# The first layer's low weights of 19 agents, made in four column parts of 128 columns instead of two products of 512

## The chip, the core and the metric

The kernel runs on one core of one Trainium2 chip. The metric is the device time of one execution in microseconds; lower is better. Engines are named as in the profile: PE (TensorE matmul; PEld is its weight load), DVE (VectorE), ACT (ScalarE), POOL (GpSimd) and SP (SyncE, which issues most DMAs).

## The reference

The reference is an attention over 49 agents, followed by a mixture of eight experts with the best one taken for each token:

```python
# q, k, v: (4, 11456, 128); agents: (4, 49, 128)
agent_v = softmax(scale * agents @ k.T) @ v        # 49 x 128 per batch
x = softmax(scale * q @ agents.T) @ agent_v        # 45824 tokens x 128
e_idx = argmax(x @ w_gate, axis=1)                 # eight experts
for e in range(8):                                 # tokens of expert e
    h = maximum(x[mask] @ w1[e], 0.0)              # 128 x 1024
    out[mask] = gate_w * sigmoid(x @ w_output_gate)[e] * (h @ w2[e])
```

## The kernel before, in words

There are four batches of 11456 tokens. For each batch the kernel computes the agents' values (49 rows of 128). It then picks the expert that most tokens of the batch should choose (`choose`, L878), and folds the agents' values into that expert's first layer: W = agent_v @ w1[e], 49 x 1024. With it a token's hidden values come from its 49 attention weights, and x itself is never formed. Tokens that chose another expert are collected in leftover tiles of 128 and computed again with their own expert: 13 such tiles for batches 0 to 2 and one for batch 3 (`left_static`, L1643). A scatter writes their rows over the first result (`left_scatter`, L1675); it begins for a phase only when all main tiles of the phase are stored.

W is made in float32 and then split into a high and a low part of float16. The tile `ad` (128 columns) holds the agents' values as its columns: 49 for the high part, the same 49 again for the low part, and the first 30 columns of the 49 last ones, so that one product with 128 rows serves three combinations of high and low. The remaining 19 agents (`AR`, 49 - 30) need another product. They lie in the tile `ar` of before in four groups of 32 columns, 19 of them filled, so that the 19 rows turn up four times, at partitions 0, 32, 64 and 96. `products` (L954) makes four products for each batch, each 128 rows by 512 columns: for each half of the 1024 columns one with `ar` and one with `ad`. Each takes a bank of PSUM, named aw. `first` (L971) turns each bank into float16: ACT writes the scaled high part (whi), DVE subtracts and writes the weights (w). The result of an `ad` bank is kept with that of the `ar` bank of its half (`rest`) in `state[b]["w"]`.

A main tile is 512 tokens. `mm1` (L1216) computes one half of its hidden values: four products h with the weights of `ad`, into four banks, and then four more that add the 19 agents, one in each group of 32 partitions of `rest`. Group g reads only its own 128 columns of the 512, at partitions 32g to 32g + 18 (L1230). `relu` splits the hidden values into a high and a low part (hh on ACT, hl on DVE), and `mm2` multiplies both with the second layer's weights vv into y. `finish` (L1270) adds the two parts of y (ACT ys, DVE os), and `store` (L1287) scales on POOL and issues the store to out on SP.

The order of the work is planned while the program is written. A `Clock` (L56) keeps a virtual time for each engine, with a cost for each instruction (`cost`, L169). `main_stream` (L1301) writes the main products and calls `tick` (L465) between them, which lets waiting streams of small work add an instruction when the plan says that its operands are ready. If nothing of the main stream is ready, `idle` (L510) adds small work or a product `warm` without a use. A change of cost anywhere changes the plan of all that comes later. Each engine then runs its instructions in the order written.

In batch 0 nothing of the main stream runs until its weights are there. There `products` uses banks of its own for the first two products, and waits after the first one until the sum of squares of w1 (mw_r) has been written; that sum sets the scale s1 (`first_scale`, L849). A similar sum, mv_r, sets the scale of the second layer (`second`, L998).

Of the kernel before, what the change touches and what calls it, by code (L numbers as in the profile page):

```python
# [7 lines left out]
F32 = mybir.dt.float32  # L8
F16 = mybir.dt.float16
# [257 lines left out]
def agent_attention_top1_moe(ctx, tc, qT, kT, v, aT, wg, wo, w1, w2, cst, out):  # L267
# [31 lines left out]
    def bank(name, dt=F32, w=512, k=None):  # L299

        k = last[0] = first_free()[1] if k is None else k
        t = ps.tile([P, w], dt, tag=f"b{k}", bufs=1, name=name)
        banks[k][1] = t.name
        return t
# [22 lines left out]
    def wait_free(long=False):  # L327
        while True:
            long_held[:] = [x for x in long_held if not banks[x[0]][0] and banks[x[0]][1] == x[1]]

            keep = clk.started and (long or not (Y or resting[0]))
            if n_free() > keep and not (long and len(long_held) > 1) and first_free()[0] <= clk.now() + 50.0:
                return
            yield None
# [43 lines left out]
        e16s.append(t)  # L378
    avd = []
    for i in range(2):  # L380
        t = cp.tile([P, 2, P], F32, name=f"avd_{i}")
        POOL.memset(t[:, 1, :], 0.0)
        avd.append((t[:, 0, :], t[:, 1, :].rearrange("p (g a) -> p g a", g=G4)))
    gss = []
    for i in range(2):
        t = cp.tile([P, 2, 18], F16, name=f"gs_{i}")
# [491 lines left out]
    def choose(b, x, ad=None, ar=None):  # L878

        sa = wk.tile([P, 1], F32, name=f"sa{b}", tag="sa")  # L880
        yield from DVE.q.tensor_reduce(sa, x, axis=AX.X, op=ALU.add)
        wgs = wk.tile([P, E], F32, name=f"wgs{b}", tag="wgs")
        yield from DVE.q.tensor_scalar(wgs, wgo[:, 0:E], sa, None, op0=ALU.mult)
        yield from wait_free()
        ga = bank(f"ga{b}")
        mark = hold()
        yield from PE.q.matmul(ga[:, 0:E], ones, wgs, start=True, stop=True)
        if ad is not None:
            yield from ACT.q.copy(ad[:, A:2 * A], ad[:, 0:A])
            yield from ACT.q.copy(ad[:, 2 * A:P], ad[:, AR:A])  # L890
            yield from POOL.q.tensor_copy(ar[:, :, 0:AR], ad[:, 0:AR].unsqueeze(1).broadcast_to([P, G4, AR]))
        gm1 = wk.tile([P, 2], F32, name=f"gm1{b}", tag="gm1")
        yield from DVE.q.tensor_reduce(gm1[:, 0:1], ga[:, 0:E], axis=AX.X, op=ALU.max)
        r1 = wk.tile([P, E], F32, name=f"r1{b}", tag="r1")
        yield from DVE.q.scalar_tensor_tensor(r1, ga[:, 0:E], gm1[:, 0:1], rank8, op0=ALU.is_ge, op1=ALU.mult)
        release(mark)
        yield from DVE.q.tensor_reduce(gm1[:, 1:2], r1, axis=AX.X, op=ALU.max)
        ei = wk.tile([P, 1], I32, name=f"ei{b}", tag="ei")
        yield from DVE.q.tensor_scalar(ei, gm1[:, 1:2], -1.0, float(E), op0=ALU.mult, op1=ALU.add)
        picking[0] = True  # L900
        urgent[0] = False
        state[b] = dict(w=[], vv=[])
        if ad is not None:
            spawn(gates(b, ad), -1)
        yield from SY.wait(ei)
        er = nc.values_load(ei[0:1, 0:1], engines=[SP], min_val=0, max_val=E - 1,
                            skip_runtime_bounds_check_because="eight minus a rank of one to eight")
        w1t = wk.tile([P, F], F32, name=f"w1t{b}", tag="w1t", bufs=2)
        yield from SY.q.dma_start(w1t, w1[bass.ds(er, 1)].rearrange("a p f -> p (a f)"))
        w2t = wk.tile([P, F], F32, name=f"w2t{b}", tag="w2t", bufs=2)  # L910
        yield from SY.q.dma_start(w2t, w2[bass.ds(er, 1)].rearrange("a p f -> p (a f)"))
        if b == 0:
            for x in (w1t, w2t):
                clk.ready[x.name] += 1000.0
        spawn(picked(w2t), -1)
        ndom = wk.tile([P, E], F32, name=f"ndom{b}", tag="ndom")
        yield from DVE.q.tensor_scalar(ndom, rank8, gm1[:, 1:2], None, op0=ALU.not_equal)
        state[b]["ndom"] = ndom
        return w1t, w2t
# [33 lines left out]

    def products(b, ad, ar, w1t, aw, marks):  # L954

        for hf in range(2):
            for x in (ar.rearrange("p g a -> p (g a)"), ad):
                while marks and b > 0 and "s1i" not in state[b]:
                    yield None
                own_ = b == 0 and hf == 0  # L960
                if not own_:
                    yield from wait_free()
                while own_ and not banks[len(marks)][0] or b == 0 and len(marks) == 1 and "mw" not in state[b]:
                    yield None

                t = bank(f"aw{b}_{len(marks)}", k=len(marks) if own_ else None)
                marks.append(hold())
                yield from PE.q.matmul(t, x, w1t[:, hf * 512:(hf + 1) * 512], start=True, stop=True)
                aw.append(t)

    def first(b, aw, marks, s1):  # L971


        s1d = wk.tile([P, 1], F32, name=f"s1d{b}", tag="s1d")
        yield from DVE.q.tensor_tensor(s1d, s1, dup, op=ALU.mult)
        for n in range(4):
            while len(aw) <= n:
                yield None
            hi = wk.tile([P, 512], F16, name=f"whi{b}_{n}", tag="whi", bufs=2)
            w = wk.tile([P, 512], F16, name=f"w{b}_{n}", tag=f"w{n}")  # L980
            yield from ACT.q.activation(hi, aw[n], AF.Copy, scale=s1d if n % 2 else s1)
            yield from DVE.q.scalar_tensor_tensor(w, aw[n], s1, hi, op0=ALU.mult, op1=ALU.subtract)
            release(marks[n])
            if n % 2:
                state[b]["w"].append((w, rest))
            else:
                rest = w

# [227 lines left out]
    def mm1(i, hf):  # L1216

        b, u, h, pp, n = tiles[i]
        w = pp * n
        own_, rest = state[b]["w"][hf]  # L1220
        x1, x2 = (x[:, 512 * h:512 * h + w] for x in X1[b, u])
        p = []
        for g in range(G4):
            p.append((bank(f"h{i}_{hf}_{g}", k=g), hold()))
            PE.matmul(p[g][0][:, 0:w], own_[:, g * P:(g + 1) * P], x1, start=True, stop=False)
            if g < G4 - 1:
                tick()
        for g in range(G4):
            rows = slice(32 * g, 32 * g + AR)
            PE.matmul(p[g][0][:, 0:w], rest[rows, g * P:(g + 1) * P], (x2 if g else x1)[rows, :], start=False, stop=True)  # L1230
        for g in range(G4):
            spawn(relu(i, G4 * hf + g, *p[g]), 0)
        tick(0)
        block()
        if hf == 1 and 4 * h + n == UNITS[u][2]:
            for x in ("x1", "x2"):
                scored((x, b, u))
        tick(0)
# [543 lines left out]
```

## Time and profile before

| what | value |
|---|---|
| median of 3 runs | 988.72 us (988.49 to 990.02) |
| profiled execution, its time | 988.17 us |
| profiled execution, its span | 986.2 us |
| PE busy | 958.7 us (97%) |
| DVE busy | 796.4 us (81%) |
| ACT busy | 592.3 us (60%) |
| first main product h | 56.81 us |
| last main product y | 972.17 us |
| last scatter issued on POOL | 977.79 us |
| mean granted clock of PE | 0.995 |

The span runs from the first instruction to the last; the execution's time includes what lies around it. A row of the timeline gives start, duration, engine, line, operation, output and inputs, size and count, and in brackets how long the engine had been idle and what it waited for. All instructions are recorded at one line, L217, because a helper issues them; they are told apart by the names of their tiles. A float32 product is recorded as two matmuls.

### The profile page before, as it was taken

What the parts mean: (1) busy time and instruction counts of PE and PEld (TensorE: products, weight loads), DVE (VectorE), ACT (ScalarE), POOL (GpSimd) and SP (SyncE); (2) the same over time, 40 slices, a digit from 0 to 9 for tenths busy, and PEclk for the clock granted to TensorE, in tenths of its full rate; (3) what the DMA queues carried; (4) which work ended last, traced back from release to release, by engine and by line L of the source; (5) the groups of instructions that cost most, each with busy time, mean ns of one, the idle gap of its engine ahead of it and who ended that gap; (6) DMA issues with size and microseconds to landing.
All of it is one profiled execution on the core that took longest, in us unless ns stands there. A gap on an engine that the chain in (4) does not pass through costs nothing. (4 is left out here: it accounts for less than half of the span.)

```text
span 986.2 us, 37446 instructions
## 1 busy us (share of the span) xinstructions
PE 958.7 (97%) x15695; PEld 730.3 (74%) x15695; DVE 796.4 (81%) x2122; ACT 592.3 (60%) x1404; POOL 353.5 (36%) x630
## 2 busy tenths in 40 slices
PE   9999999999999999999999999999999999999996
PEld 7866777777777777776777777777777677877785
DVE  2888888889788878789888888889999867767662
ACT  2376666665756666656666666657566555655552
POOL 1113264452233455331323553522225244544121
PEclk9999999999999999999999999999999999999998
DMA  9996556645467465444557545435532335633411
GB/s 328 307 301 163 157 140 152 166 133 155 116 194 199 131 160 144 140 153 129 150 170 190 155 135 155 128 120 113 134 86 83 110 111 164 178 126 120 133 32 67
DMA packets 108897, 148.62 MB, mean 151 GB/s; under 512 B 62594, under 2 KB 71222, under 8 KB 108724
## 3 DMA queue, kind: packets, MB, share of 16 engines
q1 hardware_dynamic: 107380, 144.70, 51.4%
q8 instruction: 124, 2.03, 0.9%
q0 software_dynamic: 1344, 1.49, 0.8%
q14 instruction: 49, 0.40, 0.1%
HBM read 90.88 MB, written 35.17 MB: 128 GB/s over the span
## 5 line engine op out<-in xcount | busy, mean ns | idle before, releaser
L217 PE MATMUL y<-vv,hh 128*128 128x256 f16 (+1 forms) x2880 | 527.5, 273 | 9.0 <-DVE lL L217 3.6
L217 DVE SCALAR_TENSOR_TENSOR hl<-h,hh 128x512 f16<-128x512 f32 (+1 forms) x736 | 449.3, 668 | 95.0 <-ACT hh L217 92.8
L217 PE MATMUL y<-vv,hl 128*128 128x128 f16 (+1 forms) x2880 | 500.6, 219 | 0.8 <-DVE hl L217 0.2
L217 ACT ACTIVATE hh<-h 128x512 f16<-128x512 f32 (+1 forms) x736 | 373.4, 590 | 195.6 <-PE h L217 191.4
L217 PEld LDWEIGHTS <-hh 128*128 128x128 f16 (+1 forms) x2880 | 282.8, 98 | 60.6 <-issue 18.4
L217 PEld LDWEIGHTS <-hl 128*128 128x128 f16 (+1 forms) x2880 | 284.7, 99 | 12.9 <-issue 8.3
L217 PE MATMUL h<-x_ld,w 128*128 128x512 f16 (+1 forms) x1472 | 255.8, 377 | 1.6 <-DVE hl L217 1.0
L217 PEld LDWEIGHTS <-w 128*128 128x128 f16 x1472 | 83.5, 94 | 111.4 <-issue 75.2
L217 POOL TENSOR_TENSOR os<-os,smt 128x512 f32<-128x512 f32 (+1 forms) x92 | 95.7, 1040 | 108.5 <-DVE os L217 60.0
L217 ACT COPY ys<-y 128x256 f32<-128x256 f32 x180 | 68.3, 380 | 91.7 <-PE y L217 85.6
L217 DVE TENSOR_TENSOR os<-y,ys 128x256 f32<-128x256 f32 x180 | 75.0, 417 | 33.1 <-ACT ys L217 28.2
L217 POOL TENSOR_TENSOR e<-ef,e 128x392 f16<-128x392 f32 (+1 forms) x48 | 42.4, 884 | 68.6 <-ACT e L217 68.3
L217 POOL TENSOR_TENSOR ev<-S,km_o 128x400 f32<-128x400 f32 (+1 forms) x36 | 32.9, 914 | 62.8 <-PE av L217 62.7
L217 PE MATMUL ks<-at,k_ld 128*32 128x50 f32 (+1 forms) x2316 | 46.5, 213 | 1.5 <-DMA k_ld<-kT 0.9
L217 PEld LDWEIGHTS ks<-at,k_ld 128*32 128x32 f32 (+1 forms) x2316 | 40.0, 116 | 10.2 <-issue 7.2
L217 PEld LDWEIGHTS qs<-at,q_ld 128*32 128x32 f32 (+1 forms) x2736 | 36.5, 111 | 9.2 <-issue 7.6
L217 PE MATMUL lh<-lxs,lw_ld 128*128 128x128 f32 x224 | 42.8, 278 | 0.4 <-ACT lxs L217 0.4
L217 PE MATMUL qs<-at,q_ld 128*32 128x50 f32 (+1 forms) x2736 | 43.2, 210 | 0.0
L217 PE MATMUL ly<-lw_ld,lh 128*128 128x128 f32 x224 | 42.4, 276 | 0.0
L217 POOL TENSOR_TENSOR ll<-lL,rr 128x128 f32<-128x128 f32 (+1 forms) x48 | 20.3, 423 | 55.0 <-DVE rr L217 47.4
L217 PEld LDWEIGHTS <-x_ld 128*128 128x128 f16 x360 | 26.6, 97 | 13.7 <-issue 6.4
L217 ACT COPY S<-ks 128x400 f32<-128x400 f32 (+1 forms) x48 | 23.5, 493 | 21.9 <-PE ks L217 21.9
(250 smaller groups left out, 1015.3 us busy)
## 6 DMA issues: line engine op xcount, KB each, us to landing
v_ld<-v SPq DMA_DIRECT2D x44, 512.0 KB
q_ld<-qT SPq DMA_DIRECT2D x44, 512.0 KB
out<-os SPq DMA_DIRECT2D x88, 256.0 KB
k_ld<-kT SPq DMA_DIRECT2D x43, 512.0 KB
lw_ld<-w SPq DMA_DIRECT2D x28, 512.0 KB
efd<-ef SPq DMA_DIRECT2D x44, 200.0 KB
x_ld<-x_ld SPq DMA_DIRECT2D x132, 64.0 KB
w1t<-w SPq DMA_DIRECT2D x4, 512.0 KB
```

Of the source, the lines that this page charges most:

```text
L217: return getattr(self.eng, op)(*a, **k)
```

## The change

The 19 agents now lie in one group of 32 columns only (`ar` is 128 x 32). Their weights are made first, in one bank: eight products of 32 output rows and 128 columns. Product (hf, g) writes partitions 32g to 32g + 31 and columns 128 hf to 128 hf + 127, so the bank's first 256 columns hold for each group just the columns that `mm1` reads from it. The four groups of one half take four column parts of the array. The two products with `ad` follow. `first` has three turns instead of four, the first over 256 columns, and `mm1` reads the narrower `rest`. In batch 0 the wait for mw_r now stands ahead of the second `ad` product.

```diff
-        t = cp.tile([P, 2, P], F32, name=f"avd_{i}")
-        POOL.memset(t[:, 1, :], 0.0)
-        avd.append((t[:, 0, :], t[:, 1, :].rearrange("p (g a) -> p g a", g=G4)))
+        t = cp.tile([P, P + 32], F32, name=f"avd_{i}")
+        POOL.memset(t[:, P:P + 32], 0.0)
+        avd.append((t[:, 0:P], t[:, P:P + 32]))
...
-            yield from POOL.q.tensor_copy(ar[:, :, 0:AR], ad[:, 0:AR].unsqueeze(1).broadcast_to([P, G4, AR]))
+            yield from POOL.q.tensor_copy(ar[:, 0:AR], ad[:, 0:AR])
...
     def products(b, ad, ar, w1t, aw, marks):
 
-        for hf in range(2):
-            for x in (ar.rearrange("p g a -> p (g a)"), ad):
-                while marks and b > 0 and "s1i" not in state[b]:
-                    yield None
-                own_ = b == 0 and hf == 0
-                if not own_:
-                    yield from wait_free()
-                while own_ and not banks[len(marks)][0] or b == 0 and len(marks) == 1 and "mw" not in state[b]:
-                    yield None
-
-                t = bank(f"aw{b}_{len(marks)}", k=len(marks) if own_ else None)
-                marks.append(hold())
-                yield from PE.q.matmul(t, x, w1t[:, hf * 512:(hf + 1) * 512], start=True, stop=True)
-                aw.append(t)
+        def place_(n):
+            own_ = b == 0 and n < 2
+            if not own_:
+                yield from wait_free()
+            while own_ and not banks[n][0]:
+                yield None
+            t = bank(f"aw{b}_{n}", k=n if own_ else None)
+            marks.append(hold())
+            return t
+
+        t = yield from place_(0)
+        yield "PE", [ar, w1t], [t], 0
+        clk.vt["PE"] += TURN
+        for hf in range(2):
+            for g in range(G4):
+                PE.matmul(t[32 * g:32 * g + 32, hf * P:(hf + 1) * P], ar, w1t[:, (G4 * hf + g) * P:(G4 * hf + g + 1) * P],
+                          start=True, stop=True)
+        clk.vt["PE"] += TURN
+        aw.append(t)
+        for hf in range(2):
+            while "s1i" not in state[b] if b > 0 else hf == 1 and "mw" not in state[b]:
+                yield None
+            t = yield from place_(1 + hf)
+            yield from PE.q.matmul(t, ad, w1t[:, hf * 512:(hf + 1) * 512], start=True, stop=True)
+            aw.append(t)
...
-        for n in range(4):
+        for n, m in enumerate((2 * P, 512, 512)):
...
-            yield from ACT.q.activation(hi, aw[n], AF.Copy, scale=s1d if n % 2 else s1)
-            yield from DVE.q.scalar_tensor_tensor(w, aw[n], s1, hi, op0=ALU.mult, op1=ALU.subtract)
+            yield from ACT.q.activation(hi, aw[n][:, 0:m], AF.Copy, scale=s1d if n else s1)
+            yield from DVE.q.scalar_tensor_tensor(w, aw[n][:, 0:m], s1, hi, op0=ALU.mult, op1=ALU.subtract)
             release(marks[n])
-            if n % 2:
-                state[b]["w"].append((w, rest))
+            if n:
+                state[b]["w"].append((w, rest[:, (n - 1) * P:n * P]))
...
-            PE.matmul(p[g][0][:, 0:w], rest[rows, g * P:(g + 1) * P], (x2 if g else x1)[rows, :], start=False, stop=True)
+            PE.matmul(p[g][0][:, 0:w], rest[rows, :], (x2 if g else x1)[rows, :], start=False, stop=True)
```

The change moves instructions in three places that the prediction speaks of. The first is PE in batch 0, ahead of the first main product. Here aw are the products in question, mw_r and mv_r the two sums of squares, and lg the logits of a token tile. Before:

```order
L217 MATMUL mw_r<-sq_906,ones 128x1 x2
L217 MATMUL aw_1_1064<-w1t_900,avd_91 128x512
L217 MATMUL aw_2_1068<-w1t_900,avd_91 128x512
L217 MATMUL aw_3_1076<-w1t_900,avd_91 128x512
L217 MATMUL mv_r<-sq_910,ones 128x1
L217 LDWEIGHTS x_1_ld
L217 MATMUL lg_1_1093<-gs_95,x_1_ld 128x36
```

The product aw_0 stood further up. Of the changed kernel, PE at the same place:

```order
L217 MATMUL aw_0_909<-w1t_900,avd_91 32x128 x8
L217 MATMUL aw_1_1045<-w1t_900,avd_91 128x512
L217 MATMUL mw_r<-sq_906,ones 128x1 x2
L217 MATMUL aw_2_1069<-w1t_900,avd_91 128x512
L217 MATMUL mv_r<-sq_910,ones 128x1 x2
L217 MATMUL avn_1090<-kc,avd_91 49x128
```

One large product instead of three now stands between mw_r and mv_r, and the transposed agents' values (avn) come right behind.

The second place is DVE at the same time. Here w_0 to w_3 are the weights in the order of the banks, s_b and s_s the two steps that make a scale, and vv the second layer's weights. Before:

```order
L217 TENSOR_TENSOR s1d_1087<-s_s,kc 128x1
L217 SCALAR_TENSOR_TENSOR w_0_1090<-aw_0_909,s_s,whi_0_1089 128x512
L217 TENSOR_SCALAR s_b<-mv_r 128x1
L217 SCALAR_TENSOR_TENSOR w_1_1107<-aw_1_1064,s_s,whi_1_1106 128x512
L217 TENSOR_SCALAR s_s<-s_b 128x1
L217 SCALAR_TENSOR_TENSOR w_2_1115<-aw_2_1068,s_s,whi_2_1114 128x512
L217 SCALAR_TENSOR_TENSOR w_3_1127<-aw_3_1076,s_s,whi_3_1126 128x512
L217 SCALAR_TENSOR_TENSOR vv_0_911<-w2t_902,s_s,vv_0_911 128x4x128
```

And of the changed kernel, DVE:

```order
L217 TENSOR_TENSOR s1d_1085<-s_s,kc 128x1
L217 TENSOR_SCALAR s_b<-mv_r 128x1
L217 TENSOR_SCALAR s_s<-s_b 128x1
L217 SCALAR_TENSOR_TENSOR w_0_1088<-aw_0_909,s_s,whi_0_1087 128x256
L217 SCALAR_TENSOR_TENSOR w_1_1106<-aw_1_1045,s_s,whi_1_1105 128x512
L217 SCALAR_TENSOR_TENSOR w_2_1116<-aw_2_1069,s_s,whi_2_1115 128x512
L217 SCALAR_TENSOR_TENSOR vv_0_911<-w2t_902,s_s,vv_0_911 128x4x128
```

Both steps of the second layer's scale now stand ahead of w_0, and one step w is gone. On ACT the copy of avn, which came after all four whi and vv, now stands between whi_0 and whi_1.

The third place is PE at the end of the program. Here let, lx, lh and ly are the steps of the last leftover tile: its attention weights turned, its x, its hidden values and its result. Before, the last rows of the main part read:

```order
L217 LDWEIGHTS hl_7_21357
L217 MATMUL y_0_21401<-vv_1_15701,hl_7_21357 96x128
L217 MATMUL lx_0_21435<-let_sb_0_21431,lav_0_21316 128x128
L217 MATMUL lh_0_0_21450<-lxs_0_21447,lw_00_0_ld 128x128 x4
L217 MATMUL lh_0_1_21459<-lxs_0_21447,lw_00_0_ld 128x128 x4
L217 MATMUL ly_0_21466<-lw_00_0_ld,lh_0_0_21457 128x128 x4
L217 MATMUL ly_0_21466<-lw_00_0_ld,lh_0_1_21464 128x128 x4
```

Of the changed kernel, PE where the last of the products ly stand:

```order
L217 MATMUL y_1_21375<-vv_1_15714,hh_7_21236 128x256
L217 MATMUL ly_0_21410<-lw_00_0_ld,lh_0_1_21406 128x128
L217 LDWEIGHTS hl_7_21237
L217 MATMUL y_1_21375<-vv_1_15714,hl_7_21237 128x128
L217 LDWEIGHTS hh_7_21236
L217 MATMUL y_1_21375<-vv_1_15714,hh_7_21236 128x256
L217 MATMUL ly_0_21410<-lw_00_0_ld,lh_0_1_21406 128x128
L217 LDWEIGHTS hl_7_21237
L217 MATMUL y_1_21375<-vv_1_15714,hl_7_21237 128x128
L217 LDWEIGHTS hh_0_21301
L217 MATMUL y_0_21436<-vv_0_15712,hh_0_21301 96x256
```

The leftover tile's products now stand singly between main products, and 33 products y follow the last of them; before, all 16 followed the last y. On POOL both kernels end in the same way: three multiplications of main tiles (os) and then the scatter of the last leftover tile, which waits for the hardware queues' semaphores of the last stores and for ACT.

More of the change, by code (lines that the diff above doesn't have):

```diff
@@ L975, in first @@
         yield from DVE.q.tensor_tensor(s1d, s1, dup, op=ALU.mult)
-        for n in range(4):
+        for n, m in enumerate((2 * P, 512, 512)):
             while len(aw) <= n:
                 yield None
-            hi = wk.tile([P, 512], F16, name=f"whi{b}_{n}", tag="whi", bufs=2)
-            w = wk.tile([P, 512], F16, name=f"w{b}_{n}", tag=f"w{n}")
-            yield from ACT.q.activation(hi, aw[n], AF.Copy, scale=s1d if n % 2 else s1)
-            yield from DVE.q.scalar_tensor_tensor(w, aw[n], s1, hi, op0=ALU.mult, op1=ALU.subtract)
+            hi = wk.tile([P, 512], F16, name=f"whi{b}_{n}", tag="whi", bufs=2)[:, 0:m]
+            w = wk.tile([P, m], F16, name=f"w{b}_{n}", tag=f"w{n}")
+            yield from ACT.q.activation(hi, aw[n][:, 0:m], AF.Copy, scale=s1d if n else s1)
+            yield from DVE.q.scalar_tensor_tensor(w, aw[n][:, 0:m], s1, hi, op0=ALU.mult, op1=ALU.subtract)
             release(marks[n])
-            if n % 2:
-                state[b]["w"].append((w, rest))
+            if n:
+                state[b]["w"].append((w, rest[:, (n - 1) * P:n * P]))
             else:
```

## The prediction

> **What bounds the kernel now.** The profile's page comes first: the busy times, and then the stretches of the windows view.
>
> ```profile
> span 986.2 us, 37446 instructions
> PE 958.7 (97%) x15695; PEld 730.3 (74%) x15695; DVE 796.4 (81%) x2122; ACT 592.3 (60%) x1404; POOL 353.5 (36%) x630
> 300.00:400.00 100.00, 99.56 (x1917) 75.68 (x1907) 85.10 (x214) 65.29 (x151) 44.21 (x76) 1.00 0.61 161
> 960.00:987.00 27.00, 16.71 (x180) 14.61 (x179) 7.44 (x23) 7.64 (x21) 4.79 (x5) 0.88 0.19 66
> ```
>
> The reader sees TensorE busy 97% of 986.2 us, and 99.56 of 100 us in a middle stretch at full granted clock (1.00): there, time taken off PE comes off the span. The last 27 us are different, PE 16.71 busy. So the change has three places: the start, three batches in the PE-bound middle, and the end. The profiled execution took 988.17 us, 2 us around its span and 0.55 below the median of 988.72; I work in differences and apply them to the median. 0.2%, about 2 us, is what a measurement of this kernel can tell from no change.
>
> **The middle: products of batches 1 to 3.** The group of the first layer's products (aw), and two of them in batch 3 on PE's timeline:
>
> ```profile
> L217 PE MATMUL aw<-w1t,avd x32: 592/592/697, 50.8 to 677.5; 128*128 128x512 f32 x32
> L217 DVE SCALAR_TENSOR_TENSOR w<-aw,s_s,whi x16: 717/747/751, 54.3 to 679.7; 128x512 f16<-128x512 f32 x16
> L217 ACT ACTIVATE whi<-aw,s_s x8: 665/687/694, 53.6 to 677.0; 128x512 f16<-128x512 f32 x8
> 674.02 1.02 PE L217 MATMUL aw<-w1t,avd 128*128 128x512 f32 x2
> 674.88 0.38 PE L217 MATMUL h<-x_ld,w 128*128 128x512 f16 x1
> ```
>
> One product is two matmul records (32 records for 16). The duration of 592 ns overlaps with the next one; what a product costs the engine is start to next start, 674.88 - 674.02 = 0.86 us. Each batch loses two of them: 1.72 us.
>
> Each batch gains eight products of 32 output rows by 128 columns, four beside each other in column parts. No aw row shows that shape, but the scores (ks, qs) have it: float32, 128 rows into 32, in turn to four parts.
>
> ```profile
> 62.42 0.92 PE L217 MATMUL ks<-at,k_ld 128*32 128x50 f32 x64
> 63.27 0.28 PE L217 MATMUL y<-vv,hh 128*128 128x256 f16 x1
> 247.81 0.92 PE L217 MATMUL qs<-at,q_ld 128*32 128x50 f32 x64
> 248.77 0.29 PE L217 MATMUL g<-wgo,avd 128*128 128x16 f32 x2
> ```
>
> 64 records, 32 products of 50 columns, take 0.85 us (62.42 to 63.27) and 0.96 (247.81 to 248.77), change of array shape included. Eight products of 128 columns are 1024 columns against 1600: scaled, 0.54 to 0.61 us; the upper bound is 1.72, four parts that run one after another (16 records at a quarter of 0.43). I take 0.60, because the scores are the same shape and type and only the moving operand is longer. Saved: 1.72 - 0.60 = 1.12 us per batch, 3 x 1.12 = 3.4 us.
>
> The Trainium skill (TensorE: Matmul & The Clock Gate, Part 3: Packing small matmuls) gives 2.38x as measured for three column tiles of 512 columns. By it the eight products would be an estimated 1.72 / 2.38 = 0.72 us and the three batches 3.0 us; the scores of this trace speak for the shorter time.
>
> Two evictions of 512 columns, 0.69 us each on ACT and 0.75 on DVE, become one of 256 on each (at most the full time, at least half of it): about 1 us a batch less for both engines. Neither sets the pace by itself, and that would be worth nothing but for waits of this kind:
>
> ```profile
> PE y L217 <- DVE s_b L217: 1.0, 1, 1.0
> PE y L217 <- DVE s_s L217: 0.4, 1, 0.4
> PE y L217 <- DVE lL L217: 3.6, 5, 1.2
> ```
>
> The first lies in the boundary of batch 2, the second in that of batch 3: products of hidden values wait because DVE works through w and scale steps ahead of them. One pair whi and w less per boundary takes part of 1.4 us: I put 0.5, between 0 and 1.4. The third row is a wait that comes anywhere in the run by the accident of order; since the planner works every later step out anew, such waits may come and go, and I allow 1.5 us either way.
>
> **The start: batch 0.** PE, DVE and ACT up to the first main product:
>
> ```profile
> 52.11 0.67 PE L217 MATMUL mw_r<-sq,ones 128*128 128x1 f32 x4
> 52.65 2.82 PE L217 MATMUL aw<-w1t,avd 128*128 128x512 f32 x6
> 55.54 0.36 PE L217 MATMUL mv_r<-sq,ones 128*128 128x1 f32 x2
> 56.81 0.60 PE L217 MATMUL h<-x_ld,w 128*128 128x512 f16 x2 [0.46 <-DVE s_s L217]
> 53.45 0.16 DVE L217 TENSOR_TENSOR s1d<-s_s,kc 128x1 f32<-128x1 f32 x1
> 55.94 0.16 DVE L217 TENSOR_SCALAR s_b<-mv_r 128x1 int32<-128x1 int32 x1 [0.88 <-PE mv_r L217]
> 56.02 0.74 DVE L217 SCALAR_TENSOR_TENSOR w<-aw,s_s,whi 128x512 f16<-128x512 f32 x1
> 53.52 0.18 ACT L217 ACTIVATION_READ_ACCUMULATOR vv<-w2t 128x1 f32 x1
> 54.19 0.67 ACT L217 ACTIVATE whi<-aw,s1d 128x512 f16<-128x512 f32 x1
> ```
>
> The first h waits for w_1, which DVE makes from 56.02 on; DVE held it back for s_b, which waited for mv_r, and mv_r stood on PE behind three big products (2.82 us). Now only aw_2 is between mw_r and mv_r. mw_r is held by ACT's squares and stays; aw_2 runs 52.65 to 53.51, mv_r waits for ACT's sum until 53.70 and ends 0.36 later at 54.06, s_b and s_s end by 54.45, w_0 (256 columns, about 0.45) by 54.9. On ACT whi_0 (about 0.43) ends at 54.05, but the copy of avn now stands ahead of whi_1 and waits for the avn product behind mv_r, so whi_1 runs about 54.6 to 55.25 instead of from 54.19. w_1 then takes 55.3 to 56.05, against 56.76 before: 0.7 us, bounds 0 (DVE or ACT late elsewhere) and 1.3 (that copy costs nothing). The added wait is this copy; queued behind it are whi_1, whi_2 and all hh. The smaller clearing of avd and the copy to 19 columns lie long before and on an idle POOL: nothing.
>
> Up to the last main product this makes 3.4 + 0.5 + 0.7 = 4.6 us less.
>
> **The end.** The order puts the last leftover tile's lx, lh and ly ahead of the last 33 products y; before, they stood behind all of them. PE, ACT and POOL of before, and the DMA share in half microseconds (third column from the right: granted clock, then share and GB/s):
>
> ```profile
> 972.17 0.22 PE L217 MATMUL y<-vv,hl 128*96 128x128 f16 x1
> 972.32 0.49 PE L217 MATMUL lx<-let_sb,lav 49*128 49x128 f32 x2
> 973.16 2.05 PE L217 MATMUL lh<-lxs,lw_ld 128*128 128x128 f32 x16 [0.35 <-ACT lxs L217]
> 975.05 2.01 PE L217 MATMUL ly<-lw_ld,lh 128*128 128x128 f32 x16
> 977.15 0.37 ACT L217 ACTIVATE bigs<-ly,bigs 128x128 f32<-128x128 f32 x1 [1.30 <-PEq L1717]
> 973.39 0.61 POOL L217 TENSOR_TENSOR os<-os,smt 96x256 f32<-96x256 f32 x1 [1.75 <-DVE more L217]
> 977.79 1.04 POOL L217 DMA_INDIRECT out<-bigs,ltg_0s  x1 [3.80 <-ACT bigs L217]
> 975.00:975.50 0.50, 0.50 (x6) 0.50 (x6) 0.00 (x0) 0.25 (x1) 0.00 (x0) 1.00 0.49 139
> 975.50:976.00 0.50, 0.50 (x6) 0.50 (x6) 0.00 (x0) 0.35 (x1) 0.00 (x0) 1.00 0.07 16
> 976.00:976.50 0.50, 0.50 (x7) 0.50 (x6) 0.00 (x0) 0.00 (x0) 0.00 (x0) 1.00 0.00 0
> ```
>
> Before, two chains ran side by side from 972.32: PE's leftover (to about 977.0, then ACT to 977.52), and the last main tile (POOL done at 974.00, its store issued there, packets over by 976.0). The scatter, which by the order waits for both, came at 977.79, 5.47 us after 972.32, and the program ended 8.4 us later. Now they stand one behind the other. The leftover's work, 972.32 to 977.0 less the wait of 0.35, is 4.3 us of PE ahead of the last y. After it come 1.68 us to POOL's end, the landing of the last store, and 0.27 from release to scatter. No row gives the landing; its packets end between 975.5 and 976.0, so at least 1.6 us, and the scatter of before was released by ACT at 977.52, so at most 3.5. I take 2.6, the middle. 4.3 + 1.68 + 2.6 + 0.27 = 8.85, against 5.47: 3.4 us more, bounds 2.4 and 4.3.
>
> Sum: -4.6 + 3.4 = -1.2 us, 988.72 to **987.5 us**. The terms can miss by 1.5 (order), 1.0 (end), 0.9 (waits) and 0.6 (start); as independent errors that is 2.1 us, so this case alone reaches from 985.4 to 989.6.
>
> **Rivals.** First, the gain is kept: the scatter isn't held by the landing of the last store (its data may be tracked apart, or land at once). Then the end costs 4.3 + 1.68 + 0.3 - 5.47 = 0.8, and the sum is -3.8: 984.9 us. For it: no trace row shows this wait, ACT was the releaser before. Against: the scatter's list of waits names the stores' hardware queues in both orders. Chance 0.20.
>
> Second, slower: the four column parts don't run beside each other. Then a group costs 1.72 us and the middle saves nothing but the 0.5 of waits; in batch 0 aw_1 comes 1.1 us later and the start gains nothing; the end still costs 3.4: +2.9, 991.6 us. The point from which it decides is a group of about 1.0 us, where 3 x 0.72 + 0.5 + 0.7 equals 3.4. The 64 records in 0.85 us speak against it; for it, these parts share all 128 rows, and the moving operand differs between neighbours, while the scores of one tile reuse theirs. The Trainium skill (TensorE: Matmul & The Clock Gate, Part 3, The mechanism) says that a weight load overlaps a running matmul only where the row group differs; by that rule this rival would hold, and the ks row, 13 ns a record with a load each, doesn't agree. Chance 0.10.
>
> Third, the leftover stalls PE: before, the gather of its rows was issued 10 us before lx:
>
> ```profile
> 961.54 1.07 POOL L217 DMA_INDIRECT bigs<-efd,ltu_0s  x1 [4.42 <-issue]
> ```
>
> Its products now stand about 12 us of PE work ahead of the last y, with the planned gather a group of hidden products earlier too. If gather or DVE's index steps run late, y and h queue behind let and lx on PE: up to 2 us, +0.8 in sum, 989.5 us. Chance 0.12, with other bad luck of the new order in it. My forecast keeps 0.58.
>
> **Numbers.** Faster by over 0.2% (under 986.7): nearly all of the first rival and three tenths of the forecast, 0.36. Slower (over 990.7): most of the second rival, a third of the third and a little of the forecast, 0.16. The rest, 0.48, is no difference. The range of 8 in 10 reaches from 984.7, just beyond the first rival, to 990.3, beyond the third, and leaves out the second.
>
> **What would show it.** Eight aw records of 32 rows in about 0.6 us, start to next start; over 1.0 means the second rival. The first main h near 56.1 instead of 56.81. The last y within 0.5 us of 972, with ly ahead of it. POOL's scatter released by a store's landing, 4 to 5 us after the last y; under 2.5 means the first rival. A wait of let, lx or lh for POOL or a DMA means the third. The forecast is wrong if PE's last y comes more than 2 us from 972, or if the scatter's distance is outside 3.5 to 5.5 us.

## The result, and the profile after

The changed kernel takes **982.49 us** (median of 5 runs, 981.81 to 983.68), against 988.49 (986.24 to 990.02) for the kernel before: a ratio of 0.9948, with a 95% interval of 0.9932 to 0.9965. That is 6.0 us faster by the medians, and about 5 by the ratio. The forecast was 987.5, and the measured time lies below its range of 984.7 to 990.3. The profiled execution of the changed kernel took 981.81 us, with a span of 980.0 us, 6.2 less than before.

The page after, its busy times, and the windows view of the same middle stretch and of the last 25 us:

```profile
span 980.0 us, 37550 instructions
PE 952.6 (97%) x15740; PEld 729.0 (74%) x15740; DVE 788.2 (80%) x2118; ACT 589.7 (60%) x1400; POOL 355.3 (36%) x630
300.00:400.00 100.00, 100.00 (x2031) 76.17 (x2019) 85.82 (x213) 66.00 (x153) 46.11 (x77) 1.00 0.59 155
955.00:980.00 25.00, 12.78 (x139) 11.41 (x136) 4.01 (x14) 4.98 (x16) 3.68 (x4) 0.80 0.08 28
```

The kernel is as much bound by TensorE as before. The new group of products, by the view of the tile aw, and its place in batch 1 on PE's timeline (start, duration, then in brackets the idle time before and who ended it):

```profile
L217 PE MATMUL aw<-w1t,avd x80: 272/273/697, 51.2 to 673.0; 128*32 128x128 f32 x64, 128*128 128x512 f32 x16
L217 ACT ACTIVATE whi<-aw,s_s x4: 464/473/473, 54.0 to 669.2; 128x256 f16<-128x256 f32 x4
247.24 0.22 PE L217 MATMUL y<-vv,hl 128*128 128x128 f16 x1
247.29 0.27 PE L217 MATMUL y<-vv,hh 128*128 128x256 f16 x1
247.52 0.64 PE L217 MATMUL aw<-w1t,avd 128*32 128x128 f32 x16
248.09 0.23 PE L217 MATMUL y<-vv,hl 128*128 128x128 f16 x1
```

Sixteen records take 0.57 us from the first start to the next instruction (247.52 to 248.09). The y of 256 columns ahead of them takes 0.23 instead of the 0.11 that others take (781.71 to 781.82 in the kernel before), so the step into column parts costs another 0.12. The group is worth 0.69 us against 1.72 for the two products that it replaces, so each batch saves 1.03 us and three batches save 3.1.

The end, PE's last product and POOL's steps behind it:

```profile
967.45 0.27 PE L217 MATMUL y<-vv,hh 128*96 128x256 f16 x1
967.56 0.22 PE L217 MATMUL y<-vv,hl 128*96 128x128 f16 x1
968.77 0.61 POOL L217 TENSOR_TENSOR os<-os,smt 96x256 f32<-96x256 f32 x1 [1.40 <-DVE more L217]
972.02 0.99 POOL L217 DMA_INDIRECT out<-bigs,ltg_0s  x1 [2.64 <-SPq L1727]
```

The last y, which is now TensorE's last product, starts at 967.56, 4.6 us earlier than the last y of before, although the leftover's 4.3 us of products now stand ahead of it. The scatter waits 2.64 us behind POOL's last step, for the store, and starts 4.46 us after the last y. By the DMA share in half microseconds, the packets of that store lie between 970.0 and 971.5, just ahead of the scatter at 972.02.

Where did the time go? The product g of a batch stands just ahead of its first layer. Here is g of batches 1, 2 and 3 in before, and then in after:

```profile
248.77 0.29 PE L217 MATMUL g<-wgo,avd 128*128 128x16 f32 x2
448.86 0.29 PE L217 MATMUL g<-wgo,avd 128*128 128x16 f32 x2
668.07 0.29 PE L217 MATMUL g<-wgo,avd 128*128 128x16 f32 x2
```

```profile
247.10 0.29 PE L217 MATMUL g<-wgo,avd 128*128 128x16 f32 x2
444.70 0.29 PE L217 MATMUL g<-wgo,avd 128*128 128x16 f32 x2
663.48 0.29 PE L217 MATMUL g<-wgo,avd 128*128 128x16 f32 x2
```

The differences are 1.7, 4.2 and 4.6 us, and 8.9 at the end once the leftover's 4.3 is counted. So the gain doesn't come in three like steps at the three batches. Most of it comes between the first two, and behind the third. Measured by equal amounts of matmul work (added up from the starts of all products), the two kernels run exactly in step for long pieces, for instance 4.2 us apart all the way from 362 to 430 us. The difference changes only where one of them waits or runs at a lower clock.

TensorE's waits between 240 and 960 us, the largest, first of before and then of after, there with two smaller ones for the first layer (who waits and for whom; us in total, times, longest):

```profile
PE ga L217 <- DVE lr L217: 1.5, 1, 1.5
PE y L217 <- ACT big L217: 1.3, 1, 1.3
PE ga L217 <- DVE wgs L217: 1.1, 1, 1.1
PE h L217 <- DVE hl L217: 1.0, 4, 0.4
PE y L217 <- ACT ys L217: 1.0, 2, 0.5
PE y L217 <- DVE s_b L217: 1.0, 1, 1.0
```

```profile
PE ga L217 <- DVE lr L217: 1.3, 1, 1.3
PE aw L217 <- DVE w L217: 1.2, 2, 0.6
PE y L217 <- DVE os L217: 0.8, 1, 0.8
PE y L217 <- DVE lL L217: 0.7, 1, 0.7
PE y L217 <- DVE w L217: 0.5, 1, 0.5
PE y L217 <- DVE s_b L217: 0.2, 1, 0.2
```

The whole lists sum to 10.7 us in 16 rows and 8.0 us in 14. Few rows stay: "big" and "wgs" are gone, "s_b" is down to 0.2, and a wait of the products aw for DVE's w is new. The tile "big" belongs to the leftover and "wgs" to the choice of the expert, which the change doesn't touch; only the work around them is in another order. The waits for the first layer's own steps (w, s_b and s_s) did not shrink: 1.4 us in before, with 0.4 for s_s, and 1.9 in after.

One more piece shows in the granted clock (third column from the right) of before, in two windows of equal length, the first with the wait for "big" that ends at 781.55, the second behind it:

```profile
778.94:782.35 3.41, 2.11 (x11) 0.95 (x10) 3.05 (x8) 2.77 (x8) 0.00 (x0) 1.00 0.44 167
782.35:785.76 3.41, 3.41 (x15) 1.58 (x16) 3.34 (x11) 1.21 (x3) 0.27 (x1) 0.50 0.00 0
```

For 3.41 us TensorE ran at half clock and was busy all the time, which costs about half of that, an estimated 1.7 us. The profile of after has no such stretch before its last product.

TensorE's last record starts 9.2 us earlier (976.79 to 967.56). Of that, 3.1 is the smaller products, 2.7 the waits between 240 and 960 us, 1.7 the stretch at half clock and 0.65 the time up to 240 us at equal work. Another 0.35 is the wait of lh for lxs at the end of before, which lies behind 960 us. The remaining 0.7 is not accounted for; it may lie in waits too small to list. From TensorE's last record to the end of the span, before has 986.2 - 976.8 = 9.4 us and after 12.4: the end gave back 3.0.

### The profile page after: what moved, and what is told of

Its sections match the earlier page's. It is cut to its first block, busy times and chain, and to the rows that moved or that the text cites. A ratio compares the mean times of both kernels' runs of the same rounds, so it can differ in the third digit from the quotient of the medians.

```text
span 980.0 us, 37550 instructions
## 1 busy us (share of the span) xinstructions
PE 952.6 (97%) x15740; PEld 729.0 (74%) x15740; DVE 788.2 (80%) x2118; ACT 589.7 (60%) x1400; POOL 355.3 (36%) x630
## 5 line engine op out<-in xcount | busy, mean ns | idle before, releaser
L217 POOL TENSOR_TENSOR os<-os,smt 128x512 f32<-128x512 f32 (+1 forms) x92 | 98.6, 1071 | 124.5 <-DVE os L217 93.6
L217 POOL TENSOR_TENSOR og<-oh,ll 128x64 f32<-128x64 f32 (+1 forms) x48 | 16.0, 334 | 63.1 <-DVE oh L217 59.6
```

Of the source, the lines that this page charges most:

```text
L217: return getattr(self.eng, op)(*a, **k)
```

## Experiments

Two theories. **Order**: the work that was removed is worth the 3 to 5 us of the prediction or less, and the rest is the luck of a redrawn plan, because the planner places every later instruction anew. **Work**: shorter products and evictions make the whole gain, by waits that they spare. All medians are of several runs, beside runs of the kernel before on the same chip. The chips differ (before had medians of 988.64, 988.52 and 986.48 in the three groups of runs), so kernels of different groups are compared by their ratios to before.

| kernel | median us (lowest to highest) | ratio to before (95%) |
|---|---|---|
| old_order | 987.09 (985.80 to 990.11) | 0.9986 (0.9975 to 0.9997) |
| new_order_work_back | 984.59 (983.94 to 985.40) | 0.9956 (0.9940 to 0.9971) |
| before_cheap_plan | 993.96 (992.39 to 995.95) | 1.0049 (1.0033 to 1.0065) |
| leftover_last | 978.57 (978.29 to 978.86) | 0.9895 (0.9877 to 0.9913) |
| before_kept_warm | 987.43 (987.07 to 989.39) | 0.9994 (0.9984 to 1.0004) |
| before_turn110 | 984.60 (983.72 to 985.48) | 0.9960 (0.9946 to 0.9974) |
| before_turn95 | 995.25 (993.21 to 996.67) | 1.0071 (1.0056 to 1.0086) |
| after_turn110 | 990.09 (989.01 to 991.28) | 1.0016 (1.0006 to 1.0026) |
| old_order_turn110 | 980.36 (980.10 to 981.04) | 0.9933 (0.9919 to 0.9948) |
| old_order_kept_warm | 984.50 (983.61 to 987.37) | 0.9977 (0.9965 to 0.9989) |
| after_turn95 | 983.00 (981.80 to 983.77) | 0.9957 (0.9941 to 0.9973) |
| leftover_last_turn95 | 979.75 (978.95 to 981.13) | 0.9927 (0.9912 to 0.9943) |

**old_order: the new instructions in the old order.** The planner is charged as before, and only what it writes is the change's (clk.issue advances the planned time without an instruction):

```diff
-                yield from PE.q.matmul(t, x, w1t[:, hf * 512:(hf + 1) * 512], start=True, stop=True)
+                ins = [x, w1t[:, hf * 512:(hf + 1) * 512]]
+                yield "PE", ins, [t], 0
+                clk.issue("PE", ins, [t], PE.cost("matmul", ins, [t], {}), PE.AFTER["PE"])
+                for k in range(8 if hf == 0 else 0):
+                    h, g = k // G4, k % G4
+                    nc.tensor.matmul(t[32 * g:32 * g + 32, h * P:(h + 1) * P], ar[:, 0, :], w1t[:, k * P:(k + 1) * P],
+                                     start=True, stop=True)
```

> The change's instructions in the order of before: the planner is charged for four products of 512 columns and four evictions a batch as before, while only the eight small products, two large ones and three evictions are written. Every engine's order is that of before with instructions taken out. Theory 'order' (the removed work is worth its 1.0 us of PE in each of batches 1 to 3 and about 0.5 us at the start, the rest of the gain is the new plan's luck): PE's last record at about 973.3 us against 976.8, time 985.0 us. Theory 'work' (the shorter products themselves make the whole gain, each us taken off PE and the evictions lets others start earlier): last record at about 967.6 us as in the changed kernel, time about 979.5 us, since the end keeps the cheap form of before.

Measured 987.09, ratio 0.9986. The theory "work" falls: with the same work removed, 6 us don't come. But "order" is off as well, since even the direct saving is mostly missing. In the profile, at equal work, batches 1 and 2 gain 0.6 us each, and batch 3 loses 1.1. A stretch at half clock of the kind shown above lies there (661.4 us; this profile, of a run of 989.45 us, has two more, at 57.2 and 784.3), and the second large product waits for a bank that DVE's w frees:

```profile
679.17 1.10 PE L217 MATMUL aw<-w1t,avd 128*128 128x512 f32 x2 [0.72 <-DVE w L1003]
```

**new_order_work_back: part of the work, in the new order.** One product of 512 columns more for each batch, unplanned, ahead of the small group in its bank:

```diff
+        nc.tensor.matmul(t, ad, w1t[:, 0:512], start=True, stop=True)
```

> The changed kernel with one more product of 128x512 in each batch, unknown to the planner, into the bank that the small products then overwrite: the order is that of the changed kernel, and 0.86 of the 1.02 us that PE saved in a batch is put back. Theory 'order': 2.6 us slower than the changed kernel through batches 1 to 3, perhaps 0.3 more at the start: 985.2 us. Theory 'work': most of the gain is gone, about 988 to 990 us.

Measured 984.59, 2.1 us above the changed kernel by the medians (0.8 by the ratios, whose intervals overlap), and in the profiles its last product comes 2.1 us later (969.70 against 967.56; 0.8, 0.7 and 0.6 in batches 1 to 3). Three products of 0.86 would be 2.6. With 0.86 of each batch's 1.03 us put back, the kernel still holds 4 of its 6 us, as "order" expected.

**before_cheap_plan: the same work, planned as if it cost less.**

```diff
+                if x is not ad:
+                    clk.vt["PE"] -= 582.0
```

> The kernel before, with its own products, but the planner charged 582 ns less for each product of the 19 agents, as if it were cheap: no instruction is removed or added, only the order is drawn anew, and the leftover tile's products stand ahead of the last 55 products y. Theory 'order': PE's last record moves by more than 1.5 us against 976.8, in either direction; the end costs about 2.8 us more, so between 987 and 994 us. Theory 'work': the last record of PE stays within 1 us of the work, that is at 976.5 (the wait of 0.35 us gone), and with the dearer end the time is 991 us.

Measured 993.96. No instruction of the kernel before was changed, and the time went up by 5.3 us. A redrawn plan alone is worth that much, here in the other direction. About 3 of it is the dearer end, as expected: with the leftover's products ahead of 55 y, the profile has 12.4 us from TensorE's last record to the end of the span, where before has 9.4. The rest came earlier; the last record itself is 4.8 us later (981.60 against 976.79), in the profile of a run of 995.79 us.

**leftover_last: the changed kernel with the last leftover tile's lh and ly held until all main products are written.**

```diff
+        mains_written.append(True)
...
+                yield None
+            while ph == len(PHASES) - 1 and not mains_written:
```

> The changed kernel, where the last leftover tile's lh and ly wait until all main products are written: at the end the order is that of before again (64 y, then lh and ly), all else is unchanged. If the end is as predicted, with the scatter held by the landing of the last store: the last y 3.8 us earlier than in the changed kernel (about 963.8 us), the scatter about 4.9 us behind it and released by ACT, the time 3.3 us less than the changed kernel: 979.2 us. If the landing isn't what holds the end: no difference from 982.5 us beyond 0.5. Theories 'order' and 'work' both expect the first.

Measured 978.57, 3.9 us below the changed kernel by the medians (3.5 by the spans of the profiles, 980.0 and 976.5, and 5 by the ratios) and faster than both kernels, with a ratio of 0.9895 to before. Here ACT's step behind ly releases the scatter again, as in before:

```profile
963.84 0.22 PE L217 MATMUL y<-vv,hl 128*96 128x128 f16 x1
965.74 2.01 PE L217 MATMUL ly<-lw_ld,lh 128*128 128x128 f32 x16
968.48 1.00 POOL L217 DMA_INDIRECT out<-bigs,ltg_0s  x1 [2.81 <-ACT bigs L217]
```

The scatter starts 4.64 us after the last y, with the leftover's products in between, where the changed kernel has 4.46 with nothing in between. So the leftover's time lies almost wholly beside the store's landing. This confirms the prediction's account of the end, 3.4 us, at 3.5 to 3.9 and at 5 by the ratios, whose intervals are about 1.7 us wide to either side.

**before_kept_warm: long waits filled.** 26 idle products in three waits of before, in its order (the 8 for ga here, 10 more behind pbs):

```diff
+        for _ in range(8 if b in (1, 3) else 0):
+            nc.tensor.matmul(ga[:, 256:512], idle_w, idle_x, start=True, stop=True)
```

> The kernel before, in the same order, with 26 products of ones (128 rows, 256 columns of 16 bits, results never read) put into three long waits of TensorE: 8 ahead of the ga product of batch 1, 8 ahead of that of batch 3, 10 behind pbs of the last leftover tile. Theory 'clock' (the half-clock stretch at 782 us is the answer to the wait ahead of it): the granted clock stays at 1.00 in the slices behind all three waits, TensorE's last record comes about 1.7 us earlier than 976.8, the median is 1 to 2 us lower than before's 988.6, about 987, and the runs lie closer together (under 3 us from lowest to highest, before 4.4). Rival 'chance' (the stretch has nothing to do with the wait): median and spread as before, 988.6, or slightly more.

In the profiled execution the clock did what "clock" said. The two windows of its profile around the third place show no half clock:

```profile
779.00:782.00 3.00, 2.90 (x19) 1.63 (x17) 3.00 (x9) 2.20 (x7) 0.00 (x0) 1.00 0.30 116
782.00:786.00 4.00, 4.00 (x40) 3.06 (x39) 3.93 (x10) 2.99 (x7) 0.40 (x1) 1.00 0.02 4
```

The runs were also closer together, 2.3 us from lowest to highest against 4.2 for the 21 runs of before beside it. But TensorE's last record came only 0.8 us earlier (976.00) where 1.7 were expected, the median fell by only 1.1, and the interval of the ratio takes in no change. Three of the 11 runs lay at 989; their mean granted clocks, 0.998, 0.997 and 0.997, are those of the other eight, so nothing on record says that half clock made them longer. Among the 21 runs of before beside it, the five with a mean granted clock of 0.998 have a median of 987.27, close to the 987.43 here. This run supports the clock's part, and doesn't prove its size in the medians.

**before_turn110, before_turn95, after_turn110: the same kernels under other plans.** One number of the planner is changed, what it adds at a change of array shape; no instruction is added or removed.

```diff
-    PART, TURN = 32, 100.0
+    PART, TURN = 32, 110.0
```

> The kernel before with one number of the planner changed, what it adds to TensorE's planned time at a change of array shape (100 to 110 ns): the same instructions in another order. Theory 'order' (a redrawn plan is worth several us by itself): of this run and before_turn95 at least one is more than 2 us away from 988.6, on either side. Rival 'work' (order is worth little, the change gained by the work that it removes): both within 1 us of 988.6.

> As before_turn110, with 95 ns in place of 100, and with two ly products of the leftover behind the last y. Theory 'order': of the two at least one more than 2 us away from 988.6. Rival 'work': within 1 us of 988.6.

> The changed kernel with the planner's 110 ns in place of 100, which also puts the last leftover tile's lx, lh and ly behind all y, as before has them. Theory 'order': the change's own instructions are worth 3.5 to 5 us, the rest of its 9.2 up to the last main product was this one plan's; with another plan and the cheap end it lies at 984 +- 3, and its distance from before_turn110 is another than 9 us. Rival 'work': 9 us below before_turn110, about 979.5, as leftover_last has it.

The kernel before takes 984.60 under one plan and 995.25 under the other. "Work" had put both within 1 us of 988.6, and falls. With before_cheap_plan these are four plans of the same work over a range of 1.1%, or 10.7 us. A good part of it is the clock. The profile of before_turn95 has three stretches at half clock ahead of its last product (at 660.8, 783.6 and 892.9 us) and that of before_turn110 has none: an estimated 5 us, at 1.7 each, of the 8.2 by which their spans differ (991.3 and 983.1). The runs agree: the mean granted clock was 0.989 to 0.992 in those of before_turn95 and 0.997 or 0.998 in those of before_turn110. And the changed kernel under the plan of 110 is slower than before, 990.09, and 5.5 us slower than before_turn110. Its main products were the earliest of the three plans tried, and then its end went wrong. PE's last steps:

```profile
961.59 0.22 PE L217 MATMUL y<-vv,hl 128*96 128x128 f16 x1
971.11 0.42 PE L217 MATMUL let<-kc,bigs 128*49 128x128 f32 x1 [9.30 <-DMA bigs<-efd,ltu_0s]
973.03 3.78 PE L217 MATMUL lh<-lxs,lw_ld 128*128 128x128 f32 x16 [0.36 <-ACT lxs L217]
```

And POOL's gather of the leftover rows in the same kernel:

```profile
967.43 1.06 POOL L217 DMA_INDIRECT bigs<-efd,ltu_0s  x1 [3.74 <-issue]
980.33 1.01 POOL L217 DMA_INDIRECT out<-bigs,ltg_0s  x1 [11.85 <-ACT bigs L217]
```

"Order" had expected 984 ± 3, and missed. The last y is at 961.59, but the gather of the leftover's rows is issued only at 967.43, and TensorE waits 9.3 us for it. Then lh takes 3.78 us where before had 2.05, at half clock. This is the prediction's third rival, the late gather, at 9.3 us where up to 2 were allowed, in a plan that the prediction didn't speak of.

**old_order_turn110 and old_order_kept_warm: the direct saving, again at a fixed order.**

> The change's instructions in the order of before_turn110 (the planner is charged as if nothing were removed): against before_turn110 (984.60 us) only the work differs. Theory 'order': the change's own work is worth 3 to 5 us where nothing is drawn anew, so 981 (979.6 to 981.6) here, while before to old_order had 1.5 because a wait of TensorE for w and stretches at half clock took the rest. Rival 'nothing direct' (waits take the saving back in any order): within 1.5 us of 984.6.

> old_order with the 26 idle products of before_kept_warm at the same three places. Compared with before_kept_warm (987.43 us) it is the change's work in before's order, with the granted clock at 1.00 behind the long waits in both. Theory 'order' with the clock's part: 984.5 (983 to 985.5), since old_order's profile had half-clock stretches at 57.3, 661.5 and 784.3 us, the last two behind waits that are filled here. Rival 'nothing direct': 986 to 987.5, the waits of batch 3 take the saving back.

Both pairs share the order and differ in the work alone. For 110 the ratio is 0.9933 / 0.9960 = 0.9973 (2.7 us), with the idle products 0.9977 / 0.9994 = 0.9983 (1.7 us), and the first pair gave 0.9986 (1.4 us). The expected 3 to 5 us for 110 are reached by the plain difference of the medians, 4.2, but that is over two chips and two us of it are the chips'; for the other pair 984.5 is hit, with the same reserve. "Nothing direct" doesn't hold either: in all three pairs the new instructions are faster. The profiles of the pair at 110 show where. First before_turn110, then old_order_turn110, g of batches 2 and 3 and the last y:

```profile
451.41 0.29 PE L217 MATMUL g<-wgo,avd 128*128 128x16 f32 x2
666.62 0.29 PE L217 MATMUL g<-wgo,avd 128*128 128x16 f32 x2
968.48 0.22 PE L217 MATMUL y<-vv,hl 128*96 128x128 f16 x1
```

```profile
450.76 0.29 PE L217 MATMUL g<-wgo,avd 128*128 128x16 f32 x2
459.33 1.12 PE L217 MATMUL aw<-w1t,avd 128*128 128x512 f32 x2 [1.38 <-DVE w L1003]
665.12 0.29 PE L217 MATMUL g<-wgo,avd 128*128 128x16 f32 x2
964.22 0.22 PE L217 MATMUL y<-vv,hl 128*96 128x128 f16 x1
```

Up to batch 2's g the new instructions gain 0.65 us, and from there to batch 3's another 0.85, less than 1.03 each. At the boundary of batch 2 TensorE now comes to DVE's w before it is ready: the row of 459.33 waits 1.38 us for it, where the second large product of batch 2 in before_turn110 had waited 1.02 for another step of DVE (lL). From batch 3 on 2.8 more come, in sum 4.3 us in this profile, and 2.7 by the ratios of the medians.

**after_turn95 and leftover_last_turn95.**

> The changed kernel with the planner's 95 in place of 100; its end is that of the changed kernel, 33 y behind the last ly. Theory 'order': somewhere between 980 and 993, and its distance from before_turn95 (995.25) is another one than those at 100 (-6.1) and 110 (+5.5). Rival 'work': 6 us below before_turn95, 989.

> after_turn95 with the last leftover tile's lh and ly written after all main products, as leftover_last. Expected from both: 3 to 4 us below after_turn95, as leftover_last was 3.9 below the changed kernel. If not, what a place of the leftover is worth hangs on the plan too.

The changed kernel under the plan of 95 has a ratio of 0.9957, against 1.0071 for before_turn95: 0.9887, or 11 us. So the same change is worth -0.5% at 100, +0.6% at 110 and -1.1% at 95. Holding the leftover back gave another 3.25 us, on the same chip, as expected; only the end's part repeats from plan to plan. None of these plans beats leftover_last by its ratio.

## Why the prediction was wrong

- **The small group.** Right. It was put at 0.60 us and takes 0.57, plus 0.12 of a step that wasn't counted. Three batches gave 3.1 instead of 3.4.
- **The second rival, parts one after another.** Refuted: that would have been 1.72 us for a group. The Trainium skill (TensorE: Matmul & The Clock Gate, Part 3: Packing small matmuls, The mechanism) lets a weight load overlap only where the row group differs. Here all parts share their rows, and 16 records with a load each took 0.57 us; the trace doesn't agree with that rule.
- **The start.** Right in kind and size. The first h came at 56.46 instead of 56.81, with the group of products beginning 0.43 us later by chance of the run (51.24 against 50.81), so 0.78 net; 0.7 was said. It waited for DVE's w, as said. In the changed kernel 0.65 of it is still there at 240 us; at a fixed order it isn't kept (below).
- **The end.** Right. The scatter was held by the landing of the last store and started 4.46 us after the last y, where 1.68 + 2.6 + 0.27 = 4.55 was taken; the end cost 3.0 us between the two profiles and 3.5 to 3.9 by leftover_last, where 3.4 was said. The first rival, the kept gain, fell near the measured time with the wrong mechanism; it needed a scatter within 2.5 us of the last y.
- **The step that failed** is the term for order: "since the planner works every later step out anew, such waits may come and go, and I allow 1.5 us either way". Up to the last main product 4.6 us were forecast and 8.9 measured, and the last y came 4.6 us from 972, where more than 2 was the prediction's own sign of being wrong. What is missing is in waits that have nothing to do with the first layer, and in one stretch at half clock. The clock had no term at all, although the table before the prediction gives its mean as 0.995. Four plans of the kernel before lie 10.7 us apart and three of the changed one from 0.9948 to 1.0016. The term had to be about 5 us either way, and with it the range would have been some 10 us wide and the chances of faster and slower both real.
- **A smaller miss** lies beneath it. At a fixed order the change is worth 1.4 to 2.7 us by ratio, where start and middle were put at 4.6 (the end of those orders is that of before). The prediction took a product that leaves TensorE as time that leaves the span, because TensorE was busy 99.56 of 100 us. At a batch's boundary that isn't so: TensorE reaches DVE's w sooner and waits there (0.72 and 1.38 us in the rows above). Half a microsecond was put down as gained from shorter waits; instead TensorE's waits for w, s_b and s_s between 240 and 960 us grew, from 1.4 to 2.3 us in the first pair, from 1.4 to 2.2 with the idle products and from 1.6 to 2.4 at 110. The start's 0.7 is lost as well. Compared at the same main product (h and y are equally many in all of them), the new instructions lose 2.1, 2.0 and 0.3 us in these three pairs of profiles between the first h and 72 us, and gain 0.5, 3.3 and 4.3 from there to the last y, where 3.9 was put. In the first pair each of the two pieces holds a stretch at half clock, 1.7 us, that before doesn't have; in the second TensorE waits near the start, in old_order_kept_warm, for a load of k and ahead of qs:

```profile
58.93 1.14 PE L217 MATMUL ks<-at,k_ld 128*64 128x50 f32 x32 [0.57 <-DMA k_ld<-kT]
65.46 0.90 PE L217 MATMUL qs<-at,q_ld 128*64 128x50 f32 x23 [0.88 <-issue]
```

The DMA engines were busy all through that piece (shares of 0.99 to 1.04 from 56 to 72 us), so the loads may set the pace there. No run tried that.

What is shown: that the removed work alone doesn't give 6 us (old_order), and that plans alone move both kernels by as much (the runs with other plans). What is only argued: the split of the excess into waits and half clock, and the split of the saving at a fixed order, which are read from one profile of each kernel. The two later pairs at a fixed order also compare runs on two chips.

## What to carry to other kernels

Where a planner or scheduler redraws everything behind a change, first measure what a redraw alone does: change a number that touches no work, two or three times, and take that spread as the uncertainty of every forecast. Judge a change at a fixed order beside that, and look for its gain in the stage where the shortened engine meets its next wait, since time that leaves a busy engine there can be partly waited again. A step at the end that repeats from plan to plan, like the leftover behind the last products, is worth more than a saving that the next plan takes back.

## What the runs showed of the hardware that was not expected

The granted clock fell to half in stretches of 3.41 us in the midst of the run, behind waits much shorter than that. Windows of this length, counted from the beginning of such a stretch, in before (the wait for ga at 660.42, split between two windows), in old_order (the wait for ga at 661.15) and in after (the one at 655.83):

```profile
656.06:659.47 3.41, 2.83 (x27) 1.63 (x24) 3.34 (x9) 2.54 (x8) 2.52 (x7) 1.00 0.71 245
659.47:662.88 3.41, 2.46 (x28) 2.23 (x29) 3.41 (x9) 1.05 (x4) 0.78 (x2) 1.00 0.00 1
```

```profile
658.04:661.45 3.41, 1.90 (x21) 1.26 (x20) 3.38 (x5) 2.29 (x6) 2.94 (x7) 0.99 0.24 93
661.45:664.86 3.41, 3.41 (x24) 2.69 (x23) 2.36 (x7) 0.00 (x0) 0.00 (x0) 0.51 0.02 5
```

```profile
652.66:656.07 3.41, 2.06 (x21) 1.20 (x19) 3.38 (x6) 2.29 (x7) 3.12 (x8) 1.00 0.33 127
```

The stretches lie on a fixed grid: in old_order they begin at 57.24, 661.40 and 784.28 us, and the distances of 604.16 and 122.88 us are 177 and 36 times 3.413. The same kind of wait, about 1.5 us long, brought half clock in old_order, where it lay within one window, and none in before, where the boundary split it. Lying within one window isn't enough, though: in after the wait, 1.35 us long, does so as well, and the clock stayed at 1.00. TensorE's busy time doesn't tell the cases apart either, 2.11 and 1.90 us in the windows ahead of the stretches of before (782.35) and old_order (661.4) and 2.06 in the window of after. What decides stays open. The Trainium skill (TensorE: Matmul & The Clock Gate, Part 1: The HAM clock gate) states a free-running window of 3413 ns, and the length agrees; it also says that the clock falls after a whole idle window, and there the traces disagree: by its busy time in the rows above TensorE was idle for 1.30 and 1.51 of the 3.41 us ahead of the stretches.

If the windows run on by themselves, it is chance in each run whether a wait falls into one or across two. That would explain why runs of before lie over 4 us apart and the four of leftover_last within 0.6. The mean granted clocks of the runs fit it, although they take in the time behind the last product too: of the 21 runs of before beside before_kept_warm, the five at 0.998 took 987.01 to 988.07 us and the seven at 0.994 or less 988.55 to 991.19. But no run tried the place of the windows by itself.
